# A cosformer attention feeding a gated two-layer network on one core: the first batch's attention by head halves, two late fifth tiles of q, and a new order table

## The chip, the cores and the metric

The kernel runs on one core of a Trainium2 chip. The metric is the device time of one execution in microseconds (us), less is better. Engines are named as in the profile: PE (matrix multiply; PEld its weight loads), DVE, ACT, POOL, and SP, which does nothing but issue transfers. Transfers ("DMA") are issued by SP, by POOL and, a few, by ACT, and run on 16 DMA engines.

## What is computed

```python
# q, k, v: [8 batches, 8 heads, 576 tokens, 64]; theta = pi/2 * position / 576
phi(x) = concat(relu(x) * cos(theta), relu(x) * sin(theta))        # 128 features
kv  = phi(k)^T v            # per batch and head, 128 x 64
z   = sum over tokens of phi(k)
x   = phi(q) kv / (phi(q) z + 1e-6)     # [4608 tokens, 512], heads side by side
h   = x @ w_in              # 512 -> 2048
out = (h * cos(h)) @ w_out  # 2048 -> 512
```

The dense part takes nearly all of the multiplications; the attention is small, but stands ahead of it in each batch.

## The kernel before, in words

**Tiles.** A batch's 576 tokens are cut into four full tiles of 128 (t = 0 to 3) and a fifth (t = 4) of 64. The fifth tiles of two neighbouring batches share one 128-row tile, and the eight fifths together form a ninth block of 512 tokens beside the eight batches' own blocks of 512. Dense work goes block by block (c = 0 to 8): `layer1(c)` makes h and the gate (matmuls at L528 for the first two blocks, L560 and L664 later; on ACT the sine at L501, on DVE the product at L503), `layer2` multiplies by w_out (L783 for block 0, L858 later). Blocks 0 and 1 are done plainly; later ones use a seven-product scheme for parts of both layers, whose sums (`w_out_sums` L806, `w_in_sums` L600, `layer1_sums` L621) run on DVE.

**Attention of a batch.** `load` (L316, L319) brings q, k and v, each in two transfers: one for the rows that hold five tokens (640 KB), one for the rows that hold four (512 KB). `prep` (ACT L343, DVE L344) makes phi of one tile; `cast_v` (ACT L357, DVE L358, POOL L359) casts v; `kv` (L370) sums over all five tiles; its result is copied to `kvz`; `num` (L431) multiplies phi(q), transposed, by it; the norm (DVE L447, L449, L451) divides; x is transposed for the dense part. The transposes of phi(q) and x are done on PE for batches 0 and 1 (`q_pe` L399, `x_pe` L471), by SP transfers later (`q_dma` L409 into qT, `x_dma` L481 into xT; x of batch 2 on PE).

**Weights.** w_in comes in four quarters of 512 columns (L953, POOL transfers that cast to fp16), w_out in four quarters too (L967). Transfers are held back by tiny POOL copies that write one element of the destination and read something that must have come first: `hold` (L947) makes w_in wait for k of batch 0; `hold_raw` (L972) makes batch 1's loads wait for one quarter of w_in (`GATE1`, quarter 2); `hold2` (L957) makes w_out wait for w_in's quarter 0; `part_of_w_out` (L979) makes w_out's quarters 2 and 3 wait for q of batch 1.

**Order.** Every step is added to a plan with the data it reads and writes. Two tables at the top of the file, `STARTS` and `ENGS`, give each step a place and an engine; `run` sorts by `STARTS` and emits, so each engine works through its own steps in that fixed order and waits where its data is missing. Nothing is rearranged at run time. The costs, due times and "late" weights in the step calls do not enter the program; only the two tables do.

**The start.** `first_attention` runs warm-up matmuls (L942), loads q, then k, then v (v in two head halves of four heads), and does the first batch's attention; `layer1(0)` follows. Between them and `layer2_plain(0)`, `late_q0` makes phi of the fifth q tile of batch 0 and transposes it on PE (L399). Then `second_attention` does batch 1. In the table before, w_in's quarters are issued in the order 2, 0, 1, 3, and the fourth stands behind a `hold_raw`.

**The later batches.** From batch 2 on, SP's list mixes the six loads of a batch with five transposes of phi(q) and four of x. SP issues them one after another, and a step that can't be issued yet holds up all behind it.

Of the kernel before, what the change touches and what calls it, by code (L numbers as in the profile page):

```python
# [18 lines left out]
    0, 53, 106, 0, 0, 71, 136, 201, 266, 331, 396, 461, 940, 1080, 1170, 990, 1662, 1904, 2064,  # L19
    1934, 607, 607, 797, 886, 733, 691, 888, 1346, 649, 669, 751, 817, 775, 731, 842, 1481, 934,  # L20
    997, 1064, 1039, 1163, 1081, 1216, 1123, 1002, 955, 940, 1191, 1126, 1258, 1225, 1165, 1284,
    1309, 1335, 1272, 1309, 1302, 1378, 1441, 1452, 1547, 1510, 1674, 1560, 1810, 1845, 1523, 1535,
    1559, 1646, 1736, 1770, 1833, 1797, 1894, 1845, 2022, 2084, 1711, 1723, 1779, 1912, 1947, 1935,
    2034, 2104, 2045, 2144, 2214, 2271, 2370, 2440, 2183, 2283, 2353, 2358, 2457, 2527, 2532, 2631,
    2701, 2445, 2544, 2614, 2619, 2719, 2789, 2794, 2893, 2995, 2707, 2806, 2934, 2881, 2980, 3056,
    3101, 3200, 3270, 3014, 3125, 3195, 3188, 3312, 3382, 3363, 3486, 3556, 3275, 3536, 3617, 2892,
    2850, 2968, 3030, 1752, 1792, 1857, 2044, 2084, 2952, 3689, 3719, 3809, 2024, 1642, 3017, 3082,
    3147, 3212, 3485, 3362, 4076, 3586, 3443, 3648, 3678, 3424, 3331, 3250, 3720, 3772, 3884, 3956,
    3762, 3710, 4148, 4218, 3846, 3884, 4102, 4194, 3888, 3983, 4363, 4490, 3804, 4119, 4318, 4375,
    4118, 3946, 4050, 4045, 3930, 4025, 4082, 4143, 4181, 4169, 4194, 4256, 4330, 4447, 4434, 4561,  # L30
    4684, 4719, 4410, 4422, 4446, 4657, 4819, 4720, 4707, 4784, 4948, 5010, 4645, 4632, 4669, 4925,
    4960, 4971, 5343, 5379, 5627, 5662, 3539, 3834, 3712, 4390, 3930, 4440, 4460, 4769, 4753, 5003,
    5455, 5671, 7278, 7188, 5170, 5816, 5824, 6060, 9378, 7368, 5083, 5182, 5526, 4996, 5095, 5178,
    5737, 5923, 5999, 5650, 5749, 5877, 5367, 5605, 5938, 6171, 6271, 6341, 5997, 6097, 6167, 6084,
    6209, 6279, 6470, 6629, 6786, 6383, 6517, 6587, 6557, 6741, 6847, 6879, 7027, 7116, 6756, 6865,
    6950, 6978, 7077, 7177, 7287, 7413, 7532, 7065, 7363, 7593, 4889, 5064, 8120, 9186, 4136, 4201,
    4331, 4266, 4396, 4461, 5232, 5356, 5484, 5281, 5480, 5239, 5418, 5294, 5323, 5542, 6030, 5860,
    5970, 6321, 6259, 6395, 5732, 5587, 5792, 5799, 5861, 5943, 5774, 6147, 6295, 5629, 5973, 6420,
    6228, 6035, 6675, 6644, 6657, 6681, 6856, 6915, 6843, 6966, 7011, 7177, 7313, 7153, 7165, 7238,
    7399, 7463, 7387, 7375, 7427, 7597, 7631, 6463, 7667, 7842, 6669, 7200, 7513, 7422, 7509, 7781,  # L40
    8356, 8262, 8522, 9043, 8002, 8917, 9155, 9288, 9375, 9726, 9487, 9661, 9787, 9866, 11601, 9834,
    9922, 10021, 11781, 11691, 7743, 7867, 7998, 7830, 7979, 8059, 7916, 8091, 8234, 8089, 8188,
    8295, 8176, 8362, 8512, 8349, 8474, 8573, 8435, 8534, 8634, 8609, 8707, 8837, 8806, 8993, 9064,
    8720, 8819, 8898, 9091, 9205, 9405, 9177, 9379, 9604, 9005, 9553, 9665, 9575, 9958, 10044, 9748,
    9846, 9983, 10034, 10195, 10295, 5562, 5627, 6545, 6610, 6165, 6230, 6965, 7385, 7189, 7127,
    6679, 6455, 7251, 7343, 6567, 6908, 7078, 6968, 7458, 7619, 7681, 8584, 7681, 7917, 7999, 8029,
    7956, 8124, 7743, 8238, 8320, 7805, 8300, 8575, 8412, 8644, 8791, 8708, 8695, 8732, 8916, 8893,
    8905, 8959, 9082, 9276, 9263, 9300, 9423, 9463, 9475, 9499, 9622, 10009, 10120, 10157, 10655,
    6402, 9125, 9848, 9922, 10483, 10691, 10988, 10145, 10487, 10601, 10877, 10977, 11453, 12461,
    11164, 11337, 11630, 11623, 11953, 12326, 11778, 12281, 12697, 12664, 12752, 13128, 14121,  # L50
    14211, 12926, 13057, 13250, 14301, 14614, 10262, 10389, 10356, 10597, 10232, 10307, 10275,
    10422, 10501, 10630, 10443, 10551, 10660, 10716, 10704, 10805, 10834, 10927, 11006, 11112,
    11064, 11294, 11392, 10574, 10766, 10866, 10747, 11244, 11331, 11493, 11680, 11783, 11251,
    11518, 11680, 11108, 11406, 11424, 11514, 11780, 12225, 11579, 11730, 11735, 11830, 11865,
    11949, 11909, 12010, 12240, 12347, 12040, 12128, 12286, 12108, 12550, 12636, 12194, 12500,
    12575, 12578, 12836, 12973, 12368, 12724, 12912, 7445, 7510, 8510, 8726, 7575, 8445, 9317, 8869,
    8470, 8931, 9429, 9491, 9603, 9093, 9255, 8757, 9578, 9468, 9318, 10381, 10319, 10878, 10133,
    9665, 10215, 9896, 10071, 10340, 9727, 10105, 10530, 10816, 10357, 10963, 10245, 10651, 11153,
    10964, 11151, 11226, 11349, 11468, 11480, 11575, 12092, 11722, 11710, 11844, 11967, 12096,
    12083, 12120, 12243, 13189, 13364, 13539, 13578, 13690, 13794, 13491, 13777, 13994, 14372,  # L60
    13951, 14094, 14299, 14566, 14853, 15094, 14436, 14678, 15228, 15248, 15422, 15666, 17419,
    17219, 15509, 15640, 15876, 15946, 16036, 12800, 12879, 12846, 13095, 12839, 12894, 12882,
    13034, 13362, 13653, 13013, 13069, 13144, 13200, 13188, 13303, 13404, 13478, 13596, 13819,
    13447, 13906, 14116, 13231, 13744, 13933, 13318, 13956, 14055, 14281, 14846, 14924, 13865,
    14560, 14652, 14050, 14106, 14237, 14311, 14734, 14985, 14194, 14249, 14392, 14448, 14523,
    14591, 14766, 14821, 15008, 15114, 14809, 14896, 15046, 15113, 15211, 15434, 14940, 15261,
    15373, 15336, 15702, 15877, 15026, 15311, 15938, 9747, 9877, 11088, 10898, 9812, 10465, 12071,
    12066, 12004, 10938, 11942, 11456, 11741, 11568, 11880, 11344, 11491, 11321, 11431, 12454,
    12516, 13412, 12944, 12774, 13026, 13300, 13119, 13382, 12438, 12662, 12744, 12178, 12758,
    13637, 12600, 12376, 14454, 13678, 13665, 13714, 13837, 14181, 14038, 14206, 14329, 14380,  # L70
    14367, 14486, 14961, 14654, 14666, 14713, 14836, 15224, 15199, 15561, 16086, 15999, 16146,
    16443, 16254, 16441, 16544, 16341, 16572, 16671, 17857, 16659, 16746, 16845, 16915, 17129,
    17161, 17862, 17987, 17317, 17516, 17801, 18080, 18167, 18534, 19296, 19206, 17949, 18255,
    18584, 18654, 18744, 19116, 20038, 15528, 15495, 15844, 16113, 15596, 15652, 15727, 15783,
    16110, 16382, 15938, 16060, 15895, 15950, 16210, 16321, 16068, 16260, 16408, 16557, 16528,
    16594, 16732, 15982, 16494, 16671, 16112, 16721, 16793, 16877, 17223, 17409, 17075, 17173,
    17243, 16833, 16957, 16963, 17027, 17441, 17796, 17032, 17273, 17273, 17329, 17473, 17735,
    17404, 17632, 17851, 17971, 18037, 18092, 18162, 17603, 17937, 18085, 17690, 18142, 18223,
    18385, 18484, 18631, 17776, 18254, 18509, 12433, 12368, 13507, 13572, 12869, 13151, 13844,
    14672, 13534, 15144, 15289, 14610, 14006, 14349, 13682, 13472, 14504, 14011, 13951, 15833,  # L80
    15771, 16000, 15361, 14946, 15443, 14784, 14498, 15086, 15814, 15752, 15896, 15331, 14882,
    16496, 16222, 16284, 17336, 16198, 16428, 16854, 16977, 17007, 17019, 17088, 17211, 17249,
    17261, 17304, 17733, 17448, 17460, 17485, 17608, 18725, 18961, 19374, 18944, 19316, 19415,
    18856, 19229, 19670, 20203, 19558, 19689, 19788, 19948, 19858, 20130, 20217, 20316, 19987,
    20373, 20940, 20787, 20874, 21110, 21574, 21484, 21048, 21135, 21234, 21394, 21304, 22607,
    22697, 18284, 18359, 18434, 18692, 18342, 18428, 18472, 18570, 18746, 18839, 18639, 18696,
    18683, 18796, 18813, 18900, 19031, 19086, 19165, 19488, 19099, 19251, 19707, 18727, 18918,
    19208, 19143, 19620, 19768, 19801, 20192, 20500, 19403, 19838, 19934, 19490, 19545, 19931,
    19995, 20242, 20647, 19645, 19720, 20086, 20142, 19887, 20317, 20304, 20378, 20579, 20708,
# [93 lines left out]
def kernel(  # L183
# [801 lines left out]
    def first_attention():  # L985
# [4 lines left out]
        for nm in ORDER0:  # L990
            load(0, nm, 0, HALVES if nm == ORDER0[2] else (slice(0, H),))
# [135 lines left out]
```

## Time and profile before

| what | us |
|---|---|
| three runs | 283.99, 283.96, 285.28; median 283.99 |
| the profiled execution, its own time | 284.86 |
| its span in the trace | 282.8 |
| lies around the span | 2.06 |
| PE busy in the span | 270.5 |
| DVE / ACT busy | 241.8 / 208.9 |
| first matmul of `layer1(0)` (L528) | at 20.75 |
| first matmul of `layer2_plain(0)` (L783) | at 36.17 |
| first matmul of `layer1(1)` (L528) | at 50.86 |

The profile's page says how long each engine was busy, the chain of work that ended last, and the costliest groups. The trace can be asked for any stretch: busy time per engine, the instructions in order of time with the idle time ahead of each and what ended it, and the transfers with the time from issue to landing. An engine's idle time costs something only if it is the one that the end hangs on at that place; and PE, which is busy nearly all the time, counts warm-up matmuls as busy too.

### The profile page before, as it was taken

Reading aid. Unit: us, or ns where it says so; the run is one execution under the profiler, and the core shown is the slowest. Engines: PE = TensorE matmul, PEld = TensorE weight load, DVE = VectorE, ACT = ScalarE, POOL = GpSimd, SP = SyncE. Lnnn points to the kernel's source line nnn. Section 1 sums busy time; section 2 is a strip of 40 time slices with the busy share of each in tenths; the row PEclk is TensorE's granted clock in tenths of the full one; section 3 lists DMA queues with packets and bytes.
Section 4 is the critical chain, followed back from the end, with each engine's and each line's share of the span. In section 5 each row is a group of like instructions: output and inputs, shape, how many; then the busy total and the mean of one; then the engine's idle time right before and its main releaser. Section 6 shows DMA issues by size and latency. Waiting matters only on the chain.

```text
span 282.8 us, 6698 instructions
## 1 busy us (share of the span) xinstructions
PE 270.5 (96%) x2643; PEld 210.2 (74%) x2643; DVE 241.8 (85%) x451; ACT 208.9 (74%) x363; POOL 57.8 (20%) x87
## 2 busy tenths in 40 slices
PE   6789999999999899999999999999999999999994
PEld 2468947679955577777777787787778888776883
DVE  2975897999997789998999899999999879977752
ACT  2766897898998887798989697996555687676220
POOL 1412020030500400410042023205201360330410
PEclk9999999999999999999999999999999999999999
DMA  6999999999999979999999999959583975694424
GB/s 214 302 206 253 268 258 244 352 255 214 239 294 205 286 185 297 183 312 235 271 232 322 110 333 251 231 97 205 104 140 105 188 141 74 167 126 79 101 82 154
DMA packets 83390, 58.79 MB, mean 208 GB/s; under 512 B 46368, under 2 KB 80416, under 8 KB 83360
## 3 DMA queue, kind: packets, MB, share of 16 engines
q1 hardware_dynamic: 72128, 40.77, 61.5%
q0 software_dynamic: 10496, 17.04, 29.6%
q10 hardware_dynamic: 736, 0.57, 0.6%
q8 instruction: 20, 0.33, 0.5%
q14 instruction: 10, 0.08, 0.1%
HBM read 36.74 MB, written 11.80 MB: 172 GB/s over the span
## 4 chain that ended last, share of the span: by engine, by line
PE 74%; DMA 16%; ACT 4%; DVE 3%; issue 2%; POOL 0%; SPq 0%; DVEq 0%; POOLq 0%
PE M L858 28%; PE M L664 10%; PE M L560 10%; PE M L528 9%; DMA qT<-KQ 8%; PE TR L664 4%; PE M L783 4%; DMA w_in_sb<-in_moe_w_in_dram 3%; PE TR L560 3%; DMA km<-in_k_dram 3%; PE ATT L431 3%; PE ATT L370 2%; ACT KQ L343 2%; DMA xT<-x 2%; ACT ch L501 1%
## 5 line engine op out<-in xcount | busy, mean ns | idle before, releaser
L858 PEld LDWEIGHTS <-gT 128*128 128x128 f16 x560 | 54.2, 98 | 8.7
L501 ACT ACTIVATE ch<-M 128x512 f32<-128x512 f32 x85 | 49.6, 595 | 13.1 <-PE M L560 5.3
L503 DVE TENSOR_TENSOR gT<-M,ch 128x512 f16<-128x512 f32 x78 | 51.4, 683 | 8.1 <-ACT ch L501 8.0
L858 PE MATMUL M<-w_out_sb,gT 128*128 128x256 f16 x448 | 56.0, 273 | 0.0
L343 ACT ACTIVATE KQ<-qm,CS 128x512 f16<-128x512 f32 x55 | 37.9, 718 | 6.3 <-DMA qm<-in_q_dram 4.2
L560 PE MATMUL M<-xT,w_in_sb 128*128 128x512 f16 x160 | 38.8, 379 | 0.4 <-DVE gT L503 0.4
L343 ACT ACTIVATE KQ<-km,CS 128x512 f16<-128x512 f32 x55 | 37.6, 724 | 1.3 <-DMA km<-in_k_dram 1.3
L869 ACT ACTIVATE ost<-M 128x512 f32<-128x512 f32 x41 | 24.1, 597 | 18.4 <-PE M L858 14.5
L560 PEld LDWEIGHTS <-w_in_sb 128*128 128x128 f16 x224 | 21.4, 98 | 18.5 <-issue 0.6
L359 POOL CAST V<-vm 128x1024 f16<-128x1024 f32 (+1 forms) x18 | 16.0, 912 | 90.8 <-DVE KQ L344 27.7
L858 PE MATMUL M<-T,S 128*128 128x256 f16 x256 | 32.3, 272 | 0.0
L528 PE MATMUL M<-xT,w_in_sb 128*128 128x256 f16 x256 | 30.0, 273 | 0.6 <-DVE gT L503 0.3
L858 PEld LDWEIGHTS <-S 128*128 128x128 f16 x256 | 24.6, 98 | 4.0
L528 PEld LDWEIGHTS <-w_in_sb 128*128 128x128 f16 x256 | 24.5, 98 | 3.9 <-DVE gT L503 0.6
L664 PEld LDWEIGHTS <-w_in_sb 128*128 128x128 f16 x216 | 20.6, 98 | 3.4 <-issue 0.2
L451 DVE TENSOR_TENSOR x<-ATT,rec 128x512 f16<-128x512 f32 x32 | 22.1, 691 | 1.1
L431 PEld LDWEIGHTS <-qT 128*128 128x128 f16 x320 | 15.5, 98 | 5.4 <-DMA qT<-KQ 1.7
L729 POOL DMA_DIRECT2D out_dram<-ost x20 | 11.1, 560 | 35.3 <-ACT ost L869 19.0
L676 DVE TENSOR_TENSOR Z<-M,Z 128x512 f32<-128x512 f32 x26 | 17.7, 683 | 0.6 <-PE M L664 0.6
L672 ACT ACTIVATE Z<-M 128x512 f32<-128x512 f32 x22 | 13.1, 598 | 6.8 <-PE M L664 4.2
L431 PE MATMUL ATT<-kvz,qT 128*128 128x65 f16 x288 | 16.0, 194 | 1.7 <-DMA qT<-KQ 0.9
L664 PEld LDWEIGHTS <-WS 128*128 128x128 f16 x144 | 13.7, 98 | 4.9 <-DVE XS L621 0.9
(145 smaller groups left out, 460.6 us busy)
## 6 DMA issues: line engine op xcount, KB each, us to landing
out_dram<-ost POOLq DMA_DIRECT2D x38, 256.0 KB, 4.6
qm<-in_q_dram SPq DMA_DIRECT2D x8, 640.0 KB, 6.4
km<-in_k_dram SPq DMA_DIRECT2D x8, 640.0 KB, 7.4
qm<-in_q_dram SPq DMA_DIRECT2D x8, 512.0 KB, 6.4
km<-in_k_dram SPq DMA_DIRECT2D x8, 512.0 KB, 6.2
vm<-in_v_dram SPq DMA_DIRECT2D x6, 640.0 KB, 6.1
vm<-in_v_dram SPq DMA_DIRECT2D x6, 512.0 KB, 6.5
w_in_sb<-in_moe_w_in_dram POOLq DMA_DIRECT2D x4, 512.0 KB, 9.2
```

The source lines that it names most:

```text
L343: fn = {"ACT": lambda: nc.scalar.activation(out=out_, in_=in_, func=AF.Relu, scale=sc), "DVE": lambda: nc.vector.tensor_scalar(out=out_, i ...
L359: "POOL": lambda: nc.gpsimd.tensor_copy(out=out_, in_=in_)}
L431: nc.tensor.matmul(bank[hb][:, hh * D1:(hh + 1) * D1], lhsT=a[:, h, :], rhs=z[:, h, :], start=(i == 0), stop=(i == len(parts) - 1))
L451: nc.vector.tensor_tensor(out=split(x16[n][:, hs, :], k), in0=A[:, :, :, 0:D], in1=split(rec[n][:, hs], k).unsqueeze(3).broadcast_to((P, k ...
L501: act(0.5, due, lambda: nc.scalar.activation(out=ch[c], in_=bank, func=AF.Sin, bias=math.pi / 2.0, scale=1.0), [key], [("ch", c)])
L503: mul(due, 0.61, lambda q: q.tensor_tensor(out=dst, in0=bank if len(dst.shape) == 2 else bank.rearrange("p (j s) -> p j s", j=dst.shape[1] ...
L528: nc.tensor.matmul(M1[m][:, jj * 2 * P:(jj + 1) * 2 * P], lhsT=w_in_sb[:, cc, j * P:(j + 1) * P], rhs=X[:, cc, ts], start=(cc == 0), stop= ...
L560: nc.tensor.matmul(M, lhsT=w_in_sb[:, cc, j * P:(j + 1) * P], rhs=X[:, cc, :], start=(cc == 0), stop=(cc == NCT - 1))
L664: nc.tensor.matmul(bank[0][:, j * TH:(j + 1) * TH], lhsT=a(cc, j), rhs=b[:, cc, :], start=(first and j == 0 and cc == 0), stop=(last and j ...
L676: dve(0.61, due + 0.3, lambda: nc.vector.tensor_tensor(out=dst, in0=bank[0], in1=dst, op=ALU.add), [bank[1], key], [key])
L858: nc.tensor.matmul(bank[0][:, tt * MH:(tt + 1) * MH], lhsT=a[:, j, tt * P:(tt + 1) * P], rhs=b[:, j, :], start=(first and (apart or tt == ...
L869: act(0.5, due, lambda: nc.scalar.activation(out=dst, in_=view(bank), func=AF.Copy), [bank[1]], dk)
```

## The change

- **First batch by head halves.** k of batch 0 is loaded in two halves of four heads like v. The steps that make phi(k) are cut in halves (20 of half the width in place of 10), and so are the reads of `kvz` in `num`: the first four heads' product no longer waits for the second half's `kvz`. For tiles 0 and 1 the norm is two steps of four heads (`apart`). Phi of q and k and the casts of v of this batch may now stand on DVE or ACT, as the table says. The PSUM banks of `num` and `x_pe` change.
- **Fifth q tiles later.** The first q loads of batches 0 and 1 leave out the fifth tile (512 KB each instead of 640). Two more transfers of 128 KB bring both fifth tiles, behind all other loads of batch 1. `late_q0` moves behind them.
- **Weights.** `hold` waits for the second half of k; the quarters of w_in are issued 0, 1, 2, 3 in a row; batch 1's loads wait for quarter 1.
- **The tables** `STARTS` and `ENGS` are replaced as a whole. They were searched with a model in which SP's queue of transfers is limited. The numbers given to `put`, `store` and `accum`, and `LATE_BY`, served that search and are not in the program.

Both programs have the same number of PE instructions; SP has four transfers more.

In the built program SP's list from batch 1 on reads as follows (before, then after; k, q, v are loads of a half, qT and xT transposes of a tile):

```
batch 1, before: k k q | q v v v v            (the second q waits for DVE's late_q0 step)
batch 1, after:  k k q q v v v v | q5 q5      (q5: the fifth tiles)
batch 3, before: k k v | qT0 qT1 qT2 v q qT3 q qT4 xT xT xT xT k v k
batch 3, after:  k qT4' k qT0 qT1 v q qT2 q qT3 qT4 v xT xT xT k xT k    (qT4': of batch 2)
```

`layer2_plain(0)` is eight pieces of eight matmuls. PE's list around batch 1, after: pieces 1 to 4 with two q transposes among them, kv, the other q transposes with `late_q0` among the first `num` steps, the `num` steps of tiles 0, 1 and 2 with no piece between them, piece 5, the other `num` and x transposes, piece 6, the last x transpose, and then `layer1(1)`. Before: pieces 1 to 3, kv, q transposes, `num` of tiles 0 and 1, piece 4, `num` and x transposes, piece 5, x transposes, `layer1(1)`.

```diff
-    LATE_BY, LATE_W = (0.0, 1.0, 3.0, 1.0), 0.6
+    LATE_BY, LATE_W = (0.0, 0.8, 1.8, 0.5), 0.6
     ORDER0, ORDER1, HOLDW, W_FIRST = "qkv", "kqv", 1, None
-    GATE1 = (w_in_sb[0:2, 0, Dff // 2 + 1:Dff // 2 + 2], [("w_in", 2)])
+    HOLD0, ORDER_W = ("k", [HB], [0]), (0, 1, 2, 3)
+    GW = 1
+    GATE1 = (w_in_sb[0:2, 0, GW * Dff // 4 + 1:GW * Dff // 4 + 2], [("w_in", GW)])
...
-    def load(b, nm, due, hs=(slice(0, H),)):
+    def load(b, nm, due, hs=(slice(0, H),), ts=(0, NT + 1)):
...
-                nc.sync.dma_start(out=blocks(m, n)[:, h], in_=five)
+                nc.sync.dma_start(out=blocks(m, n)[:, h, t0:t1, :], in_=five[:, :, t0:t1, :])
...
-                nc.sync.dma_start(out=blocks(m, 1 - n)[:, h, 0:NT, :], in_=four)
+                nc.sync.dma_start(out=blocks(m, 1 - n)[:, h, t0:NT, :], in_=four[:, :, t0:NT, :])
...
-            pe(HB * len(parts), MMA, due, lambda hb=hb: mm(hb), rd, [keys[hb]])
+            pe(HB * len(parts), MMA, due, lambda hb=hb: mm(hb), [x for x in rd if x[0] != "kvz" or x[2] == hb], [keys[hb]])
...
+        segs = list(zip(N, cut))
+        if apart:
+            for i, x in enumerate(segs):
+                dve(0.74, due, lambda x=x: norm([x]), [keys[i]], [("x16", n, i)])
+            return n
...
-                in_=raw[ORDER0[1]][0:2, 0, 0, 0:1].broadcast_to((2, 4)))
-        pl.add("POOL", 0.4, 0.5, 0, hold, hk(ORDER0[1], [0], [0]), [("w_in", g) for g in range(4)])
-        for g in range(4):
+                in_=raw[HOLD0[0]][0:2, HOLD0[1][0], 0, 0:1].broadcast_to((2, 4)))
+        pl.add("POOL", 0.4, 0.5, 0, hold, hk(*HOLD0), [("w_in", g) for g in range(4)])
+        for g in ORDER_W:
...
-        for nm in ORDER0:
-            load(0, nm, 0, HALVES if nm == ORDER0[2] else (slice(0, H),))
+        load(0, "q", 0, ts=(0, NT))
+        load(0, "k", 0, HALVES)
+        load(0, "v", 0, HALVES)
...
-        for t in range(NT + 1):
-            prep(0, "k", t, 0, "DVE", 4)
-            prep(0, "k", t, 1, "DVE" if t == 2 else "ACT", 4)
-        for hb in range(2):
+        for hs in HALVES:
             for t in range(NT + 1):
-                cast_v(0, t, "ACT" if t % 2 else "DVE", 5 + hb, HALVES[hb])
+                for g in range(2):
+                    prep(0, "k", t, g, "", 4, hs)
+            for t in range(NT + 1):
+                cast_v(0, t, "", 5, hs)
...
-            num(0, t, 8 + t, PAIRS0[t % 2])
+            num(0, t, 8 + t, (att, (BANKS[0], BANKS2[0]), BANKS2, att)[t], t < 2)
...
-            load(1, nm, T, HALVES if nm == ORDER1[2] else (slice(0, H),))
+            load(1, nm, T, HALVES if nm == ORDER1[2] else (slice(0, H),),
+                 (0, NT) if nm == "q" else (0, NT + 1))
...
+        for b in range(2):
+            load(b, "q", T, ts=(NT, NT + 1))
+        late_q0()
...
     first_attention()
     layer1(0)
-    late_q0()
     second_attention()
```

## The prediction

> **What bounds the kernel now.** I read the page first, then a table of stretches, then the instructions in order of time and the transfers.
>
> ```profile
> span 282.8 us, 6698 instructions
> PE 270.5 (96%) x2643; PEld 210.2 (74%) x2643; DVE 241.8 (85%) x451; ACT 208.9 (74%) x363; POOL 57.8 (20%) x87
> ```
>
> PE is busy all but 12.3 us, so only that idle time can be won, and whatever PE has to wait in addition is lost. Columns of the stretches: from:to, length, busy us and count of PE, PEld, DVE, ACT, POOL, then granted clock, DMA share, GB/s.
>
> ```profile
> 5.00:10.00 5.00, 2.27 (x29) 1.55 (x27) 2.72 (x7) 1.95 (x3) 0.00 (x0) 1.00 1.08 366
> 15.00:20.00 5.00, 4.28 (x72) 2.97 (x68) 3.54 (x14) 2.62 (x5) 1.09 (x3) 1.00 1.24 206
> 45.00:50.00 5.00, 5.00 (x60) 3.09 (x58) 4.71 (x18) 3.44 (x6) 0.00 (x0) 1.00 1.13 310
> 60.00:80.00 20.00, 20.00 (x262) 17.25 (x260) 18.70 (x36) 17.85 (x34) 5.95 (x9) 1.00 1.05 230
> 80.00:135.00 55.00, 52.41 (x503) 38.11 (x501) 49.27 (x91) 47.46 (x84) 7.81 (x11) 1.00 1.07 255
> 135.00:200.00 65.00, 65.00 (x647) 51.39 (x645) 62.42 (x111) 54.88 (x95) 14.27 (x21) 1.00 1.09 225
> ```
>
> The idle time has three places: ahead of the first dense matmul at 20.75 (what PE does before is warm-up and little else), 2.59 us between 80 and 135, and the tail after the last matmul. From 60 to 80 and from 135 to 270 PE has none. Two stretches of the order of time say why:
>
> ```profile
> 20.75 1.03 PE L528 MATMUL M<-xT,w_in_sb 128*128 128x256 f16 x8 [0.28 <-DMA w_in_sb<-in_moe_w_in_dram]
> 23.20 8.04 PE L528 MATMUL M<-xT,w_in_sb 128*128 128x256 f16 x72 [0.32 <-DVE gT L503]
> 30.79 0.60 SPq L316 DMA_DIRECT2D qm<-in_q_dram  x1
> 80.69 8.08 SPq L409 DMA_TRANSPOSE qT<-KQ  x3
> 86.28 0.49 DVE L344 TENSOR_SCALAR KQ<-km,CS 128x512 f16<-128x512 f32 x1 [0.89 <-DMA km<-in_k_dram]
> 87.42 1.02 PE L560 MATMUL M<-xT,w_in_sb 128*128 128x512 f16 x4 [0.44 <-DVE gT L503]
> 97.28 0.43 PE L431 MATMUL ATT<-kvz,qT 128*128 128x65 f16 x8 [0.91 <-DMA qT<-KQ]
> 107.87 0.61 PE L664 MATMUL M<-XS,WS 128*128 128x256 f16 x4 [0.63 <-DVE XS L621]
> 134.41 0.60 PE L664 MATMUL M<-XS,WS 128*128 128x256 f16 x4 [0.55 <-ACT Z L672]
> ```
>
> The four waits from 87 on (0.44 + 0.91 + 0.63 + 0.55 = 2.53, nearly all of the 2.59) follow late transfers: k that SP issued at 75.06 is there only at 86.28, and three q transposes take SP 8.08 us to issue (2.69 each), where one at 132.31 took 1.24. SP stands, and all in its list behind comes late.
>
> **The first batch (forecast -0.1 us).** Without the fifth tile q is 131 KB shorter; at 366 GB/s k and v land 0.36 earlier: k at 10.14 (5-token half issued 2.90, landing 7.6 later, 10.5 before), v at 13.3. That is spent again: behind k's second half ACT's list holds eleven half-width steps (0.39 each, as its three casts of v at 13.32 in 1.18) and a full one (0.65), so the last cast of v ends at 10.2 + 4.95 = 15.15. kv's second half ends near 15.9 (15.63 before), its copy on DVE (0.43) at 16.35 (16.10). Then four half norms: 0.12 + 0.20 + 0.37 = 0.69 each from the halves of the paired rows at 16.68 to 17.93, ending at 19.15; the two whole ones ended at 18.97. With 1.2 from there to the second xT, as before, that is 20.35, and in PE's list the x transpose of tile 3 still stands ahead of L528: about 20.7.
>
> w_in's quarter 0 is now the first in POOL's list, no longer the second: the first landed 5.7 after its issue at 11.15, at 16.9, the second at 20.62. So the wait for w_in (0.28) goes, and x is what is late next, at the same time. The third step of L528 waited for a PSUM bank that DVE's product at 22.45 freed (0.32 at 23.20); in the new list it has another bank and waits for xT of tile 2 instead, near 23.05. Two dense steps are done by then in both. I take -0.1. Bounds: -0.6 (both L528 waits gone) and +0.5 (v later, below).
>
> DVE's half-width phi has no row: between a half-width cast (0.22) and the full phi (0.41). I take the cast's side; at the other end DVE's nine would add 1.6, hidden behind ACT up to 15.15.
>
> A rule on the other side: the Trainium skill ("DMA: Bandwidth & Descriptors", Queues, rings and completion order) has each DMA engine take packets from its queues in turn. The trace agrees as far as it goes: between 25 and 30 POOL's queue had 62.5% and SP's 52.6% of the engines at once. By that rule w_in, issued 0.4 earlier, would slow the last of v by about as much, and the sum would be +0.3 here.
>
> **The late fifth tiles (0).** 16 PE instructions (8 transposes with loads, 0.61 us) leave 31.07 and come back near 45: nothing won in the sum. Two transfers come in addition: 0.60 each on SP and 131 KB each. They stand behind batch 1's loads and ahead of batch 2's k, which was issued at 42.48; the DMA engines ran dry before that (from 350 GB/s at 38.5 to 59 at 39.9), and that covers them. Without cover they would hold batch 2's k back by 0.7 (131 KB at 366 GB/s, twice) or, at the pace of the x transposes of that size at 96.64 (6.55 for four), by 3.3; k's first user came some 8 us after its issue, so I keep 0.7 as the end.
>
> The Trainium skill (same page, Specifications) wants runs of 512 bytes; these are of 256. No plain load of the trace is so short. [...]
>
> **Batch 1 (+0.4).** SP's second q load waited until 30.79 for DVE's late_q0, and four v loads behind it. After, all eight follow each other behind w_in's quarter 1, near 23 to 28; k starts later (18.37 before), q and v end about 38 instead of 41. PE was never short there (45 to 50: 5.00 of 5.00), so nothing is won directly; w_out's quarters 2 and 3, which wait for q, come about 3 us earlier than 38.46. Against that, no piece of layer 2 (1.73) stands any more between the num steps of tiles 0, 1 and 2. Their chain is ACT's kvz (0.60) and a norm (1.05): uncovered 1.65 at most, 0 if the q transposes there (0.62 each) cover all. I take 0.4, near the lower end, as three or four of these transposes stand there.
>
> **The transfers of the later batches (-2.1).** In the new list no three transposes follow the loads at a stretch; the half v load that stood ahead of them comes after two, and v's other half behind all five. The upper bound of the gain is all 2.59; 0 if SP stalls as before. The nearest rows are 60 to 80 and 135 to 200, where the same loads and transposes alternate more and PE waits for none. I leave one wait of 0.5. DVE, with 49.27 of 55 busy, is late next; its 5.73 idle there leave room for 2.1.
>
> The tail has the same steps after the last matmul: 0. **Sum:** -0.1 + 0 + 0.4 - 2.1 = -1.8. From the profiled execution (284.86, its span 282.8 and 2.06 around it) that is 283.06; that execution lies 0.87 above the median of the runs, 283.99, so I forecast 282.2.
>
> **Rivals.** *The waits only move* (0.25): SP has four more steps (2.4 us), as many transposes, and DMA engines that are full either way (share 1.07), so other steps come late by as much. For it: a whole new order has new places to be late, also from 135 on. Then -0.1 + 0.4 + 0: 284.3.
>
> *DVE becomes the bound, slower* (0.17). Six pieces instead of five, and a q transpose pair, stand ahead of layer1(1): 1.75 + 0.6, its first matmul near 53.5 instead of 50.86. Its 16 products on DVE (0.69) start so much later; if DVE can't fill the gap with phi of batch 2, it idles about 3 us between 45 and 55, and from 60 to 80 it has only 1.3 to catch up: 1.7 are lost, with 0.3 of the first rival: 286.0. It decides from an idle DVE of over 1.3 there. Against it: batch 2's loads, issued at 42.5, feed about twenty phi steps.
>
> *The front wins more* (0.08): the half norms let both xT come by 19.7 and L528 with them, 1 us earlier: 281.2.
>
> **Chances and range.** Forecast 0.50, rivals 0.25, 0.17, 0.08. What a measurement can tell here is 0.5%, 1.42 us. Faster by more: 0.42 of the forecast and the front's 0.08 = 0.50. Slower by more: 0.17 and 0.03 of the first rival = 0.20. Within: 0.30. Low end: -0.6 + 0 - 2.6 = -3.2, 280.8; high end 285.8, which takes in the first rival with batch 1's full 1.65 and leaves part of the second out.
>
> **What would show it.** Right: L528 first at 20.4 to 21.0 with no wait for w_in; between 80 and 135 PE idle under 1 us and no SP stretch like 8.08 for three transposes; between 40 and 55 PE idle under 1. Wrong: PE idle over 2 between 80 and 200 (first rival), DVE idle over 2 between 45 and 55 and full after (second), L528 before 20 (third). What would make it all wrong is a wait of PE from 135 to 270, where it had none.

## The result, and the profile after

The changed kernel takes 286.71 us (median of 15 runs, 285.25 to 288.29); the kernel before, run beside it on the same chip, 284.46 (283.0 to 285.95). The ratio is 1.0098, with a 95% interval of 1.0073 to 1.0123: slower by 2.8 us by the ratio (the medians are 2.25 apart), where 1.8 less was forecast. Executions of one kernel lie 3 us and more apart, so below a kernel's time is told as its ratio to the kernel before in the same group of runs.

The profiled execution took 286.58 us. Its page, of the changed kernel:

```profile
span 284.8 us, 6737 instructions
PE 272.2 (96%) x2643; PEld 210.4 (74%) x2643; DVE 242.7 (85%) x460; ACT 212.1 (74%) x370; POOL 58.1 (20%) x87
```

Its table of stretches, with the columns as in the prediction:

```profile
15.00:20.00 5.00, 3.12 (x61) 2.18 (x58) 3.92 (x16) 2.29 (x4) 0.37 (x3) 1.00 1.23 205
45.00:50.00 5.00, 4.67 (x95) 3.93 (x92) 3.56 (x11) 4.50 (x8) 0.00 (x0) 1.00 1.08 305
60.00:80.00 20.00, 20.00 (x264) 17.36 (x263) 18.62 (x37) 19.14 (x35) 6.43 (x8) 1.00 1.04 264
80.00:135.00 55.00, 53.30 (x503) 37.58 (x498) 50.36 (x90) 48.92 (x87) 7.36 (x10) 1.00 1.12 237
135.00:200.00 65.00, 64.54 (x647) 51.50 (x648) 62.15 (x113) 54.26 (x95) 13.41 (x20) 1.00 0.99 225
```

PE's busy time from 15 to 20 has fallen from 4.28 to 3.12; from 80 to 135 it has risen by only 0.89, and 0.46 of idle time has appeared from 135 on, where there was none. The order of time of PE in the changed kernel, its waits and the first dense matmul:

```profile
17.32 0.29 PE L438 MATMUL ATT<-kvz,qT 128*128 128x65 f16 x4 [1.13 <-DVE x L459]
19.47 0.29 PE L438 MATMUL ATT<-kvz,qT 128*128 128x65 f16 x4 [0.74 <-DVE x L459]
22.44 1.04 PE L541 MATMUL M<-xT,w_in_sb 128*128 128x256 f16 x8
...
48.71 0.29 PE L438 MATMUL ATT<-kvz,qT 128*128 128x65 f16 x4 [0.33 <-DVE x L459]
...
93.61 0.43 PE L438 MATMUL ATT<-kvz,qT 128*128 128x65 f16 x8 [0.65 <-DMA qT<-KQ]
129.40 1.03 PE L871 MATMUL M<-w_out_sb,gT 128*128 128x256 f16 x8 [0.22 <-ACT ost L882]
135.46 0.61 PE L677 MATMUL M<-XS,WS 128*128 128x256 f16 x4 [1.02 <-DVE XS L634]
```

(L438 is num, 431 before; L541 the first dense step, 528 before; L573 is 560, L677 is 664, L634 is 621, L871 is 858; L350 and L351 make phi, L488 copies xT.) The first dense step starts at 22.44 in place of 20.75, with no wait for w_in any more. Ahead of it stand two waits that the prediction did not have: num, which writes ATT, waits 1.13 and 0.74 us for a norm, which reads ATT. In the kernel before, num of tile 0 waited only for kvz:

```profile
16.15 0.29 PE L431 MATMUL ATT<-kvz,qT 128*128 128x65 f16 x4 [0.52 <-DVE kvz L384]
```

VectorE in the same stretch of the changed kernel:

```profile
16.10 0.43 DVE L391 CAST kvz<-M 128x260 f16<-128x260 f32 x1 [0.23 <-PE M L377]
...
16.84 0.42 DVE L459 TENSOR_TENSOR x<-ATT,rec 128x256 f16<-128x256 f32 x1
17.85 0.16 DVE L454 TENSOR_SCALAR den<-M 128x4 f32<-128x4 f32 x1 [0.58 <-PE M L438]
```

kvz's second half is there at 16.53. The second half of tile 0's num needs nothing else, but PE starts it only at 17.32, when VectorE has ended its read of the first half at 17.26; VectorE then waits 0.58 for PE. The two halves of ATT are parts of one PSUM tile, each as large as a bank of its own in the program (512 columns of fp32). The reading to be tested: a write of the tile is ordered behind a read of it, also where the two touch different halves. The written order has keys of their own for the halves, so it placed the two steps side by side. The wait at 135.46 goes back to the sync engine, whose list in the changed kernel has

```profile
122.63 0.60 SPq L321 DMA_DIRECT2D km<-in_k_dram  x1
123.33 6.17 SPq L494 DMA_TRANSPOSE xT<-x  x3
```

and VectorE's sums (L634) wait 1.18 for these xT.

### The profile page after: what moved, and what is told of

Same layout as the page of the kernel before. It is cut to its first block, busy times and chain, and to the rows that moved or that the text cites. A ratio compares the mean times of both kernels' runs of the same rounds, so it can differ in the third digit from the quotient of the medians.

```text
span 284.8 us, 6737 instructions
## 1 busy us (share of the span) xinstructions
PE 272.2 (96%) x2643; PEld 210.4 (74%) x2643; DVE 242.7 (85%) x460; ACT 212.1 (74%) x370; POOL 58.1 (20%) x87
## 4 chain that ended last, share of the span: by engine, by line
PE 81%; DMA 9%; DVE 6%; SPq 1%; issue 1%; ACT 0%; DVEq 0%
PE M L871 30%; PE M L677 11%; PE M L573 11%; PE M L541 10%; PE M L796 5%; DMA qT<-KQ 5%; PE TR L677 4%; PE ATT L438 3%; PE TR L573 3%; PE ATT L377 3%; DMA km<-in_k_dram 2%; DMA xT<-x 2%; DVE KQ L351 1%; DVE x L459 1%; DVE gT L516 1%
## 5 line engine op out<-in xcount | busy, mean ns | idle before, releaser
L871 PEld LDWEIGHTS <-gT 128*128 128x128 f16 x560 | 53.8, 98 | 9.5 <-issue 0.6
L516 DVE TENSOR_TENSOR gT<-M,ch 128x512 f16<-128x512 f32 x78 | 52.0, 684 | 6.7 <-ACT ch L514 6.4
L871 PE MATMUL M<-w_out_sb,gT 128*128 128x256 f16 x448 | 56.7, 272 | 0.2 <-ACT ost L882 0.2
L350 ACT ACTIVATE KQ<-qm,CS 128x512 f16<-128x512 f32 x56 | 38.0, 720 | 4.5 <-DMA qm<-in_q_dram 4.2
L350 ACT ACTIVATE KQ<-km,CS 128x512 f16<-128x512 f32 (+1 forms) x61 | 40.2, 690 | 1.2 <-DMA km<-in_k_dram 0.9
L573 PE MATMUL M<-xT,w_in_sb 128*128 128x512 f16 x160 | 39.5, 379 | 0.0
L573 PEld LDWEIGHTS <-w_in_sb 128*128 128x128 f16 x224 | 21.0, 98 | 16.5
L871 PE MATMUL M<-T,S 128*128 128x256 f16 x256 | 32.3, 273 | 0.0
L541 PE MATMUL M<-xT,w_in_sb 128*128 128x256 f16 x256 | 30.1, 273 | 0.0
L871 PEld LDWEIGHTS <-S 128*128 128x128 f16 x256 | 24.9, 98 | 4.1
L541 PEld LDWEIGHTS <-w_in_sb 128*128 128x128 f16 x256 | 24.7, 98 | 3.6 <-issue 0.2
L677 PEld LDWEIGHTS <-w_in_sb 128*128 128x128 f16 x216 | 20.6, 98 | 4.8 <-DMA xT<-x 0.4
L459 DVE TENSOR_TENSOR x<-ATT,rec 128x512 f16<-128x512 f32 (+1 forms) x34 | 22.3, 660 | 1.1
L742 POOL DMA_DIRECT2D out_dram<-ost x20 | 12.0, 604 | 52.8 <-DVE ost L893 31.3
L438 PEld LDWEIGHTS <-qT 128*128 128x128 f16 x320 | 15.7, 98 | 7.1 <-issue 2.9
L438 PE MATMUL ATT<-kvz,qT 128*128 128x65 f16 x288 | 16.6, 194 | 3.0 <-DVE x L459 2.2
L677 PEld LDWEIGHTS <-WS 128*128 128x128 f16 x144 | 13.6, 98 | 4.0 <-DVE XS L634 1.3
```

The lines of the kernel that those rows point to most:

```text
L350: fn = {"ACT": lambda: nc.scalar.activation(out=out_, in_=in_, func=AF.Relu, scale=sc), "DVE": lambda: nc.vector.tensor_scalar(out=out_, i ...
L438: nc.tensor.matmul(bank[hb][:, hh * D1:(hh + 1) * D1], lhsT=a[:, h, :], rhs=z[:, h, :], start=(i == 0), stop=(i == len(parts) - 1))
L459: nc.vector.tensor_tensor(out=split(x16[n][:, hs, :], k), in0=A[:, :, :, 0:D], in1=split(rec[n][:, hs], k).unsqueeze(3).broadcast_to((P, k ...
L516: mul(due, 0.61, lambda q: q.tensor_tensor(out=dst, in0=bank if len(dst.shape) == 2 else bank.rearrange("p (j s) -> p j s", j=dst.shape[1] ...
L541: nc.tensor.matmul(M1[m][:, jj * 2 * P:(jj + 1) * 2 * P], lhsT=w_in_sb[:, cc, j * P:(j + 1) * P], rhs=X[:, cc, ts], start=(cc == 0), stop= ...
L573: nc.tensor.matmul(M, lhsT=w_in_sb[:, cc, j * P:(j + 1) * P], rhs=X[:, cc, :], start=(cc == 0), stop=(cc == NCT - 1))
```

## The experiments

**Two suspects, singly and together.** Theory: the front loses by the shared tile, and the wait at 135 by the load ahead of the transposes; rivals stand in the expectations. The edits to the changed kernel:

```
own_bank:  num(0, t, ..., (att, (BANKS[0], BANKS2[0]), BANKS2, att)[t], ...)
        -> num(0, t, ..., ((att[0], BANKS[2]), (BANKS[0], BANKS2[0]), BANKS2, att)[t], ...)
x_ahead:   STARTS[902] (batch 6's k load, 655 KB)  12029 -> 12480, behind three x transposes of batch 4
both:      the two
```

(The expectations call this load batch 4's and the transposes batch 3's; in the order of the program they are batch 6's and batch 4's.)

> The changed kernel with one edit: the second half of tile 0 of num is written to a PSUM bank of its own tile (M1_2) instead of the second half of the tile ATT, whose first half the norm of the first heads is reading at that time. Theory (the front lost its 1.7 us because PE's write of one half of ATT is held until VectorE has read the other half): the waits of 1.13 us at 17.32 and 0.74 us at 19.47 before num go, VectorE's idle time of 0.58 and 0.84 us there with them, and the first dense matmul comes at 21.0 to 21.4 instead of 22.44; the time falls by 1.0 to 1.4 us, to about 285.5. Rival (the half-width steps on ScalarE and VectorE themselves are what is late, 0.35 us on VectorE where 0.23 was forecast): the first dense matmul stays within 0.3 us of 22.44 and the time within 0.4 us of the changed kernel.

> The changed kernel with one load moved in the sync engine's list: the 655 KB load of batch 4's k that was issued at 122.63, ahead of three x transposes of batch 3 (6.17 us for three), stands behind them. Theory (PE's wait of 1.02 us at 135.46 for the sums of xT comes from transposes that queue behind that load's packets): the three start 0.7 us earlier and take under 5 us, the wait falls to 0.3 us or less, and the time falls by 0.6 to 1.0 us. Rival (the transposes are slow because the engines are full with the four stores of 256 KB issued at 121.1 to 123.3): they take 5.5 us or more as before, the wait falls by at most the 0.7 us of the earlier start, and later k gives part of it back: the time falls by 0.3 us or less.

> The changed kernel with the two edits that were run singly: the second half of tile 0's num in a bank of its own, and the load of batch 4's k behind the three x transposes. Theory (two separate losses, 1.66 us in the front and 0.8 to 1.4 us at 135, add up): PE's wait of 1.44 us at 134 that the first edit alone had is under 0.3, and the time lies between 0.2% below and 0.35% above the kernel before. Rival (transfers set the pace between 70 and 135, and an earlier PE only waits longer for them): waits of 1 us or more stay at 79 and come anew between 90 and 140, and the time stays 0.5% or more above the kernel before, no better than the first edit alone.

| kernel | ratio to the kernel before | 95% interval |
|---|---|---|
| changed | 1.0098 | 1.0073 to 1.0123 |
| own_bank | 1.0053 | 1.0024 to 1.0083 |
| x_ahead | 1.0071 | 1.0043 to 1.0099 |
| both | 1.0018 | 0.9986 to 1.0050 |

The first edit takes away 0.45 and 0.53% (without and with the second), the second 0.27 and 0.35%; both together 0.80%, or 2.3 us of the 2.8. Each pair alone has overlapping intervals, so the sizes are rough; only the sum is clear. Plain medians give 0.65% for both together, and for each edit alone only 0.2 and 0.1%. PE in the run with a bank of its own:

```profile
16.45 0.67 PE L438 MATMUL M<-kvz,qT 128*128 128x65 f16 x12 [0.39 <-DVE kvz L391]
...
20.79 1.04 PE L541 MATMUL M<-xT,w_in_sb 128*128 128x256 f16 x8
...
79.61 1.89 PE L573 MATMUL M<-xT,w_in_sb 128*128 128x512 f16 x8 [1.37 <-ACT xT L488]
134.05 0.61 PE L677 MATMUL M<-XS,WS 128*128 128x256 f16 x4 [1.44 <-DVE XS L634]
```

The waits of 1.13 and 0.74 are gone, and with one operand's bank changed the first dense step comes 1.65 earlier; the rival (the half-width steps are what is late) falls. Four later profiles of the new front, without the shared write and with the clock at 1.00, have their first dense step at 20.76 to 20.95. Of the 1.65, 1.3 us reach the time by the ratios, but this share is as rough as the sizes. The sync engine in the run with the load moved:

```profile
120.93 6.33 SPq L494 DMA_TRANSPOSE xT<-x  x3
127.34 0.61 SPq L321 DMA_DIRECT2D km<-in_k_dram  x1
```

Here each theory was half right: the three transposes take as long as before (6.33), so it was not the load's packets that slowed them, but they start 2.4 earlier, as the list no longer stands before that load (2.1 us in the changed kernel, from 120.50 to 122.63), and PE's wait near 135 is gone. It goes with the place of this load in every profile of the new later order: 1.02 to 1.44 in the seven with the load ahead, none in the four with it behind. `both` did what its theory said, in the time too, but PE then waits elsewhere, 0.97 us near 93 and 0.73 near 130, as its rival had it in part.

**Joint norms.** k and v in halves, but tiles 0 and 1 of num normalised over all heads again (`apart` left out, two entries less in the table).

> The changed kernel with the norms of tiles 0 and 1 joint again (one norm over all eight heads, behind both halves of num, as in the kernel before); k and v stay in halves by heads, the order of everything else stays. Theory (the halves of the norm bring nothing: four take 0.75 us each, two joint ones 1.05 each, and with them goes the wait of PE's write on VectorE's read of the same tile): the first dense matmul comes at 20.0 to 20.6 (22.44 in the changed kernel, 20.79 with the second half in a bank of its own), and the time falls by 1.2 to 1.9 us from the changed kernel's, to 0.3 to 0.6% above the kernel before. Rival (norms by halves do bring the first x tiles forward once the banks are apart): the first dense matmul comes at 21.0 or later, and the time lies above that of the run with the bank of its own.

1.0073 (1.0044 to 1.0101). Without the shared-tile wait the first dense step comes at 20.90, hardly other than with halves and a bank of its own; the 20.0 to 20.6 of the theory was missed, as the order, laid out for halves, has PE's fill matmuls between the two halves of tile 3, and VectorE waits for them there:

```profile
19.48 0.17 DVE L454 TENSOR_SCALAR den<-ATT 128x8 f32<-128x8 f32 x1 [0.42 <-PE ATT L438]
```

So for the first dense step normalising by halves neither gained nor cost: 3.0 us of VectorE for four halves against 2.2 for two whole ones, begun 0.44 sooner. The time, between the changed kernel's and that of own_bank, tells neither apart.

**The front undone, and the fifth tiles undone.** old_front has the first batch's steps of the kernel before within the changed kernel (w_in's order, late fifth tiles and all later steps as changed); fifth_with_batch loads the fifth q tiles with their batches.

> The first batch as in the kernel before (k whole, both halves of a tile normalised together, the same order of its steps), everything else as in the changed kernel: w_in's quarters in the order 0 to 3, the late fifth q tiles, and the new order from the first dense matmul on. Theory (the front alone made the kernel slower; the rest of the new order is worth 0.3 us to the good): first dense matmul at 20.5 to 21.0, time 1.4 to 1.8 us below the changed kernel, within 0.6 us of the kernel before. Rival (what the front loses is only waited for elsewhere, and the new order of the later batches is what costs): PE waits longer at 48, 93 and 135, and the time stays within 0.6 us of the changed kernel, so 1.6 us or more above the kernel before.

> The changed kernel with the fifth q tiles of the first two batches loaded again together with the other four tiles (the two late loads are gone from the sync engine's list, the first batch's q is 131 KB longer). Theory (the late loads stand beside an idle queue and are worth nothing in the sum): the time within 0.3 us of the changed kernel, with v of the first batch some 0.36 us later and the first dense matmul up to 0.4 us later. Rival (the late loads keep the sync engine busy where it had backed up, 3.30 and 3.08 us per load between 23 and 33, and hold batch 2 back): PE's wait of 0.33 us at 48.7 goes and the time falls by 0.3 us or more.

old_front: 1.0060 (1.0026 to 1.0094), first dense step at 20.57. It falls between theory and rival, and a wait is in it that belongs to my mix of two orders: batch 1's loads were let go 1.6 us later than in the changed kernel (its first k load issued at 23.45, not 21.86), and PE waited for a phi of q:

```profile
39.82 0.62 PE L405 MATMUL M<-IDENT,KQ 128*128 128x128 f16 x8 [1.19 <-ACT KQ L349]
```

fifth_with_batch: 1.0108 (1.0060 to 1.0156), from six runs. Its first dense step came at 23.30, 0.86 later and not at most 0.4, with the granted clock at 0.64 from 18 to 22. The late fifth tiles are worth nothing that these runs can tell; the wait of 0.33 before 50 stayed, so the rival falls.

**More moves.** three_moves is `both` with PE's last x transpose of batch 2, ScalarE's copy of it to xT and VectorE's last product of `layer1(1)` moved ahead of phi steps that wait for a load (STARTS[362], [363], [299]); joint_moves is joint_norms with all the moves.

> As the run with both edits, with two more moves in the written order of steps: ScalarE's copy of batch 2's last xT tile ahead of two phi steps that wait for a q load (it stood behind them and ended at 79.5, where PE waited 1.37 us), and VectorE's last product of layer 1 of batch 1 ahead of a phi step that waits for the same load. Theory (PE's wait at 79.6 comes from a copy that is ready but stands behind steps that wait for a transfer): the wait is under 0.4 us, and the time is 0.2 to 0.5% below the run with both edits. Rival (PE then only reaches the next late transfer sooner): the wait goes, waits for transfers between 85 and 140 grow by about as much, and the time is within 0.2% of the run with both edits.

> Joint norms of tiles 0 and 1 as in the first run of this group, and the moves of the run before this one (the k load behind the three x transposes, ScalarE's copy and VectorE's product ahead of the phi steps). Theory (the losses are separate and these edits take them all away): first dense matmul at 20.0 to 20.6, PE idle under 1.5 us between 40 and 140, time 0.1 to 0.8% below the kernel before. Rival (a front that is another 0.4 us earlier is lost again to transfers): the time within 0.2% of the run with the bank of its own and the same moves.

The reason for the moves, from ScalarE's list in own_bank: the copy (L488) stood ready behind two phi steps (L350) that waited for q.

```profile
77.74 1.33 ACT L350 ACTIVATE KQ<-qm,CS 128x512 f16<-128x512 f32 x2 [2.04 <-DMA qm<-in_q_dram]
78.98 0.57 ACT L488 ACTIVATE xT<-TR 128x512 f16<-128x512 f16 x1
```

three_moves: 1.0022 (0.9995 to 1.0049), joint_moves: 1.0038 (1.0007 to 1.0068). No gain over `both`; neither beats the kernel before. joint_moves missed its theory (first dense step 20.80, PE idle 2.58 us from 40 to 160); it lies within 0.2% of three_moves, as its rival had it. The wait at 79.6 is gone, but it was also missing in `both`, which still has the old list. It was one execution's wait, and I had taken it for the list's.

**How much of a profile is one execution's?** That question also hangs over the 2.59 us which the forecast's largest term was taken from. So both kernels were profiled again without a change, and long_warm (the kernel before, `warm(14, 6.5)` made `warm(20, 6.5)`) and new_front (own_bank's first batch, with the order of the kernel before from the first dense step on) were run.

> The kernel before, unchanged, profiled a second time. Theory (the 2.59 us that PE was idle between 80 and 135 in the first profile, in an execution 0.87 us above the median, are one draw of waits that differ from execution to execution, so the forecast's gain of 2.1 us was taken from too large a stock): the idle time of PE between 80 and 135 differs by 0.5 us or more from 2.59 and lies at least partly at other steps than 87, 97, 108 and 134; in an execution near the median it is 1 to 2 us. Rival (the waits belong to the written order): four waits at the same four steps, 2.3 to 2.9 us in all, and the first dense matmul at 20.75 within 0.1.

> The kernel before, unchanged, profiled a third time. Both theories as in the run before this one: waits between 80 and 135 that differ by 0.5 us or more in sum and by place, or 2.3 to 2.9 us at the same four steps.

> The kernel before, unchanged, profiled a fourth time, to see how often the clock falls in its front. Theory: a granted clock of about 0.5 near 10 to 12 again and the first dense matmul at 21.5 to 22.7, PE idle between 80 and 135 under 1.5 us. Rival: clock 1.00, first dense matmul near 20.75 and idle time near 2.6 as in the first profile; and 3.5 us from the last VectorE instruction to the end of the span in either case.

> The kernel before, unchanged, profiled a fifth time. As in the run before this one: a granted clock of about 0.5 near 10 to 12 with the first dense matmul at 21.5 to 22.7 and under 1.5 us idle between 80 and 135, or 1.00, 20.75 and 2.6; 3.5 us behind the last VectorE instruction.

> The changed kernel, unchanged, profiled a second time. What belongs to the written order comes again: PE's wait of 1.1 us for VectorE before the second half of tile 0, the first dense matmul at 22.2 to 23.0, 0.33 us before 50, and a wait of 0.8 us or more for the sums of xT near 135. What belongs to one execution does not: the wait of 0.65 us near 93.6 and that of 0.22 near 129.4 change by a third or more, and the time from the last VectorE instruction to the end of the span (4.1 us, 3.5 in the kernel before) moves between 3.4 and 4.2 in both kernels. Rival for the last: 4.1 again here and 3.5 again in the kernel before.

> The changed kernel, unchanged, profiled a third time. As in the run before this one: the wait before tile 0's second half, the first dense matmul at 22.2 to 23.0 and the wait near 135 come again; those near 93.6 and 129.4 and the time of the last stores move.

> The kernel before with 20 warm-up matmuls of 512 columns at the start instead of 14, so that PE idles 0.3 to 1.6 us less before the first q transposes. Theory (the granted clock of 0.50 between 10 and 12 us in the second and third profile of the kernel before follows that idle time of 1.9 to 2.9 us, and puts the first dense matmul at 21.8 to 22.6 instead of 20.75): the clock stays at 1.00 up to 24, the first dense matmul comes at 20.6 to 21.2; if a front that is 1 us earlier counts in the kernel before, the time falls by 0.2 to 0.4%. Rival (the transfers between 70 and 135 take the gain back, as an execution with the first dense matmul at 20.75 took 284.86 us and one with 21.81 took 283.29): first dense matmul as early, PE idle 1 us more between 80 and 135, time within 0.15%.

> The first batch as in the changed kernel with the second half of tile 0 in a bank of its own (k and v in halves, norms by halves, w_in's quarters in the order 0 to 3), and everything from the first dense matmul on as in the kernel before, its fifth q tiles loaded with their batches. Theory (two causes: the front loses by the shared tile, and the new order of the later batches loses by itself some 1 us, since PE idled 2.5 to 2.8 us there between 40 and 160 in three profiles against 1.1 to 2.6 in the kernel before): first dense matmul at 20.6 to 21.1, PE idle between 40 and 160 in all 1.0 to 2.6 us, time within 0.3% of the kernel before or below it, and 0.3% or more below the run with the bank of its own and the new order. Rival (the new order is not worse, and the front and the end of the program make up the whole): time as in the run with the bank of its own, 0.4 to 0.7% above the kernel before.

One row for each profiled execution, in us; the clock is the lowest of the stretches 6 to 10, 10 to 14, 14 to 18 and 18 to 22, the idle time that of PE in the stretches from 40 to 160:

| execution | its time | first dense step | clock | PE idle 40 to 160 | last VectorE step ends | from there to the span's end |
|---|---|---|---|---|---|---|
| before, first | 284.86 | 20.75 | 1.00 | 2.59 | 279.30 | 3.50 |
| before_again1 | 283.29 | 21.81 | 0.62 | 1.37 | 277.99 | 3.51 |
| before_again2 | 284.03 | 22.57 | 0.63 | 1.12 | 278.73 | 3.57 |
| before_again3 | 283.42 | 21.89 | 0.71 | 1.40 | 278.13 | 3.47 |
| before_again4 | 284.21 | 21.50 | 0.78 | 2.10 | 278.91 | 3.49 |
| long_warm | 285.96 | 20.50 | 1.00 | 3.98 | 280.16 | 3.54 |
| changed, first | 286.58 | 22.44 | 1.00 | 2.49 | 280.70 | 4.10 |
| after_again1 | 286.55 | 22.45 | 1.00 | 2.83 | 280.64 | 4.16 |
| after_again2 | 286.99 | 22.91 | 0.69 | 2.79 | 281.06 | 4.14 |
| x_ahead | 285.43 | 22.98 | 0.69 | 1.12 | 279.50 | 4.10 |
| own_bank | 285.16 | 20.79 | 1.00 | 3.19 | 279.29 | 4.11 |
| both | 285.98 | 20.95 | 1.00 | 2.99 | 280.06 | 4.14 |
| three_moves | 283.62 | 20.76 | 1.00 | 1.57 | 277.62 | 4.08 |
| new_front | 286.50 | 22.90 | 0.61 | 2.55 | 280.91 | 3.79 |

The first theory holds: the same kernel before idled 2.59, 1.37, 1.12, 1.40 and 2.10 us. And the later its first dense step, the less it idled: their sum is 23.2 to 23.7 in all five. I read it so: from 80 to 135 the transfers set the pace of this kernel, and a front that is 1 us earlier is waited away. long_warm tests it: in its profile the clock stays at 1.00 and the first dense step is the earliest, at 20.50, but the idle time is 3.98, and its time, over all runs, is 1.0033 (0.9993 to 1.0072). The gain of 0.2 to 0.4% is ruled out; the rival's 0.15% lies within the interval. The 3.98 are one execution's, and that one was slower than its median of 285.33. Its PE and its sync engine:

```profile
88.08 1.02 PE L560 MATMUL M<-xT,w_in_sb 128*128 128x512 f16 x4 [1.34 <-DVE gT L503]
90.63 0.43 PE L431 MATMUL ATT<-kvz,qT 128*128 128x65 f16 x8 [1.52 <-DMA qT<-KQ]
```

```profile
80.50 9.62 SPq L409 DMA_TRANSPOSE qT<-KQ  x3
```

Against it, the third profile of the kernel before, with its first dense step at 22.57, in its sync engine's list and its stretches:

```profile
82.50 5.42 SPq L409 DMA_TRANSPOSE qT<-KQ  x3
```

```profile
10.00:12.00 2.00, 2.00 (x22) 2.00 (x21) 1.47 (x4) 0.66 (x2) 0.19 (x1) 0.50 1.09 358
80.00:135.00 55.00, 54.22 (x520) 39.53 (x516) 51.48 (x94) 49.83 (x89) 7.79 (x11) 1.00 1.09 248
```

The very three transposes that the prediction held against the old order at 8.08 us took 5.42 to 9.62 in that same order.

In the changed kernel less is waited away. own_bank's front is 1.65 earlier, and in its profile PE idles 3.19 us from 40 to 160, against 2.70 in the mean of three of the changed kernel: 0.5 more. The first dense step of own_bank, both and three_moves, 20.76 to 20.95, is also 0.8 us ahead of the mean of the five profiles of the kernel before, and still none of the three is faster than it.

What came again in all three profiles of the changed kernel: the wait for the norm before tile 0's second half (1.13 each time), the 0.33 before 50, and 1.02, 1.25 and 1.07 before the step near 135. The wait near 94 changed (0.65, 0.57, 1.04), that at 129 was not there again.

new_front did not settle what it was for. Its time is 1.0046 (1.0011 to 1.0080), but its first dense step came at 22.90, not 20.6 to 21.1: PE waited 2.88 us for q's phi, q being longer again by its fifth tile, and the clock fell.

```profile
9.83 1.01 PE L406 MATMUL TR<-IDENT,KQ 128*128 128x128 f16 x8 [2.88 <-DVE KQ L351]
```

It is a late front with a large idle time, in the old later order. So the sum of 23.2 to 23.7 belongs to the kernel before as a whole, its front included, and the share of the new later order by itself stays open.

## Why the prediction was wrong, point by point

Mean of the three profiles of the changed kernel less mean of the five of the kernel before: first dense step +0.9 (22.60 against 21.70), PE idle from 24 to 40 -0.2, from 40 to 160 +1.0 (2.70 against 1.72), end of the program +0.6; +2.3, of +2.8 between the spans. The other 0.5 is not idle time: from the first dense step on PE is busy 0.6 longer with as many matmuls (255.0 against 254.4, and 254.1 to 255.0 within the five), while 0.1 less is idle before 24. What makes it longer stays open.

**"The first batch (forecast -0.1 us)" failed.** Its chain was sized well: with the bank of its own the first dense step starts at 20.79, forecast 20.7, and w_in is not waited for. What it lacked is the order between PE's write and VectorE's read of ATT. It took its "four half norms" as independent of the writes of the other halves, because the keys of the plan are; that cost 1.65. The step was also measured from one front: 20.75 was the earliest of five of the kernel before. VectorE's nine half-width phi took 3.12, 0.35 each, not 0.22; with them VectorE's casts of v ended at 15.27 and ScalarE's at 15.08 (forecast 15.15), so they were not quite hidden. k's second half was there at 10.34 (forecast 10.14), and kvz's second half at 16.53, 0.2 later than the forecast 16.35. Of the +0.3 that the prediction worked out from the Trainium skill ("DMA: Bandwidth & Descriptors", Queues, rings and completion order), whose rule has each DMA engine serve its queues in turn, the trace shows nothing: the casts of v waited for no transfer.

**"The transfers of the later batches (-2.1)" failed, and weighed most.** The stock of 2.59 was one execution's; the mean of five between 80 and 135 is 1.44, less than the 2.1 that were to be won. In the changed kernel it is 1.51, with 0.31 more from 60 to 80 and 0.56 past 135, where there was none: +0.9 in place of -2.1. And the new order did not draw on it: no three q transposes follow each other any more, but three x transposes do, behind a load that is new there (122.63), and PE waits 1.0 to 1.25 at 135. x_ahead shows that this wait is the list's. It is part of the loss only: what holds up the steps near 94, and the late waits of `both`, was not tested.

**The late fifth tiles (0)** hold, within 0.5%. "No plain load of the trace is so short" was misread: IDENT, 32 KB over 128 partitions, comes in runs of 256 bytes too. **Batch 1 (+0.4)**: 0.33 at 48.71, as said; but four of the five profiles of the kernel before have 0.34 near 41, which the first lacked, so in the difference it is nothing.

**The tail ("the same steps after the last matmul: 0") failed by 0.6**, with the same steps: 4.10 to 4.16 from the last VectorE step on, 3.47 to 3.57 before. The last stores are issued and land alike; the rest lies behind them, and its cause stays open.

**The rivals.** "The waits only move" (284.3) was the nearest in mechanism: waits went from 87, 97 and 108 to 94 and 135. It was given -0.1 for the front, and so no place for what the shared tile cost. "DVE becomes the bound" came nearer in number (286.0), by luck, for its mechanism fell: VectorE did idle 1.44 us from 45 to 50, past the 1.3 from which it was to decide, but from 60 to 80 it still had 1.38 to spare and PE had no wait there (in the other two profiles PE waited 0.62 and 0.30 there, while VectorE idled 2.18 and 1.86). "The front wins more" fell with the front.

**What "would show it"** did its work: the first dense step past 21.0, PE idle over 2 us from 80 to 200 (2.16) and PE idle past 135 were named as signs of being wrong.

## What to carry to other kernels

Before you let a step start on one half of a tile while another engine reads the other half, look at what the order is kept by: here it is the whole PSUM tile, though each half is as large as a bank and the plan has a key for each; another tile's bank took the wait away. A search that counts the halves as free will put the two steps side by side. Profile the unchanged kernel several times before you put a price on a wait: what comes again at the same place belongs to the order, what moves belongs to that execution. And where transfers set the pace later on, an earlier front may be waited away, as in the kernel before; see over several profiles if first start plus later idle time stays the same.

## What the runs showed of the hardware

In four of five profiles of the kernel before, the granted clock of TensorE was 0.50 to 0.55 between 10 and 12 us, after PE had idled 1.94, 2.46, 2.48 and 2.92 us behind its 14 warm-up matmuls. In the first profile, after 2.73 idle, it stayed at 1.00 (the last column but two; in the line of the third profile, above, it is 0.50):

```profile
10.00:12.00 2.00, 2.00 (x19) 1.18 (x17) 2.00 (x6) 1.45 (x3) 1.04 (x2) 1.00 1.09 356
```

In before_again1 the first phi of q began only 0.20 us later than there, and the first dense step 1.06 later. With the gap filled (long_warm) the clock stayed at 1.00. Asked in stretches of 0.05 us, the traces show when it fell: 2.1 to 2.7 us after the last warm-up matmul, in three of the four while PE still idled (in before_again4 2.1 us into a gap of 2.48). It came back 3.4 us later in all four. x_ahead, fifth_with_batch and the third profile of the changed kernel show a fall to 0.50 inside a gap of only 1.13 to 1.14 us, with another of 0.81 some 2 us ahead of it, and it lasted 3.4 us there too.

The Trainium skill ("TensorE: Matmul & The Clock Gate", Part 1: The HAM clock gate) has a window of about 3.4 us that runs free of the kernel, and two rates, half and full. The traces agree on the half rate, on like gaps falling differently and, by the 3.4 us of each low spell, on the length; but the skill's table wants an idle window of that length, and here none of the falls had so long an idle time before it.

The time of a transpose's issue on the sync engine is no constant of its place in the list: the same three q transposes took 5.42, 6.22, 6.44, 8.08 and 8.14 us in five executions of one program. Where they took 8 us, the core had moved 230 and 234 GB/s between 60 and 80, in the others 264 to 277; which of the two brought the other about is not shown.
